# A recurrence's operand half loaded and half copied on chip, and a key product taken where its factor lies

## The chip, the cores and the metric

The kernel runs on one core of one Trainium2 chip. The metric is the device time of one execution in microseconds, the median of three runs.

## What is computed

The reference has three stages on float32 data. The change lies in the first, an attention with a recurrent state for each of 32 heads (4 batches of 8), 768 tokens and a head size of 40:

```python
for t in range(S):
    y[:, :, t] = np.einsum('bhd,bhde->bhe', rt, state)
    Sa = np.einsum('bhde,bhe->bhd', state, at)
    state_decay = state * wt[:, :, None, :] - np.einsum('bhd,bhe->bhde', Sa, bt)
    state = state_decay + np.einsum('bhd,bhe->bhde', vt, kt)
```

Its result, 3072 rows of 320, goes through a mixture of 8 experts of which each row takes two (routing by a noisy gate), and then through one feed-forward layer of width 2048.

## The kernel before

The recurrence is cut into chunks of 32 tokens (`C`), 24 in all (`NC`), and the 32 heads into two halves (`NP`), so that the main loop `chain(g)` has 48 steps: step g belongs to chunk g // 2 and half g % 2. A chunk's decays are folded into scaled operands, its inner dependence is a unit triangular matrix of 32 by 32 for each head, and the inverse of that matrix turns a chunk into a few matmuls.

Three generators run ahead of the chain and are interleaved with it at written-out times (`pump`). `prepare` makes a chunk's operands: `scale` forms running products of w on VectorE and multiplies a (`abd`) and k, b (`kb`) by them on GpSimd; `prods` forms the triangular matrices on TensorE, of which ScalarE takes one part to `lscr` in DRAM; `turns` transposes kb to token rows (`kn`, stored to DRAM as `knd`) and the decays to token rows (`EN`: a tile of 128 partitions holds two chunks, 64 partitions each, and for each partition two groups `ab` of heads). `scale_a` multiplies a in token rows by EN, into `AM`. `solve` takes four chunks (`GJ`) at a time: it loads lscr as `Lu`, inverts on VectorE with a few products on GpSimd, and stores the result as `tscr`. `apply` loads it as `Tbd` and multiplies AM by it, into `Zt`.

A step of the chain does `s_mm` (the state's part on TensorE with KB, scaled into the state tile ST two steps on by VectorE), `tr` (transposes of ST; ScalarE writes TRs and rows of KB), `u_mm` (Zt with ST of the next step, which ScalarE copies into ST), `y_mm` of the step before (the output, with KB and RR) and `rv_mm` (RR, masked by VectorE). KB is a tile for one chunk, two of them in turn. Its partitions 64 to 127 hold knd, for each half of the heads once for `s_mm` (index 0) and once again for `y_mm` (index 1).

Before the change `load_kb` (L494) fills both copies with one broadcast load of knd, issued in the even step of chunk i for chunk i + 1, after `y_mm`, which reads the buffer last. `load_at` (L251) loads a in the row order of AM, and `load_et` (L258) copies EN by two transfers into the same row order, so that `scale_a` (L265) is one multiply of 128 partitions; it runs two chunks behind `turns` (`LA`). `pair` (L201) loads 104 partitions of wa or kb, of which 40 to 63 are padding.

TensorE, VectorE, ScalarE and GpSimd run in the order in which the program is written. SyncE issues nearly all transfers; the order of its queue is planned by the framework from its own estimate of when each one can go, and each engine's queue is in order on the chip.

Of the kernel before, what the change touches and what calls it, by code (L numbers as in the profile page):

```python
# [11 lines left out]
F32 = mybir.dt.float32  # L12
# [17 lines left out]
NTB = 2  # L30
GJ = 4
RW = 64 + D
LA = 2


def layout_rec(inp):

    c = np.ascontiguousarray

    def heads_t(x):  # L40
        return x.reshape(NP, PR, 2, NC, C, D).transpose(3, 2, 5, 1, 0, 4)


    wa = np.zeros((NC, 2, 64, NW + 1 + 2 * PR * C), np.float32)
    w33 = np.ones((NC, 2, 64, PR, 2, C + 1), np.float32)
    w33[..., 0] = 0
    w33[:, :, :D, :, :, 1:] = heads_t(inp["w"])
    wa[..., :NW] = w33.reshape(NC, 2, 64, NW)
    wa[:, :, :D, NW + 1:] = heads_t(inp["a"]).reshape(NC, 2, D, -1)
    at = inp["a"].reshape(NP, PR, 2, NC, C, D).transpose(3, 2, 0, 4, 1, 5)  # L50
    kb = np.zeros((NC, 2, 64, PR, 2, 2, C), np.float32)
    for x, n in enumerate("kb"):
        kb[:, :, :D, :, :, x] = heads_t(inp[n])
    rt = inp["r"].reshape(NP, HH, NC, C, D).transpose(2, 4, 0, 1, 3)
    vn = np.zeros((NC, NP, C, HH, 64), np.float32)
    vn[..., :D] = inp["v"].reshape(NP, HH, NC, C, D).transpose(2, 0, 3, 1, 4)
    flat = lambda x: x.reshape(NC, 128, -1)
    rows = lambda x: c(flat(x)[:, :64 + D])
    return dict(wa=rows(wa), at=flat(c(at)), kb=flat(kb), r=c(heads_t(inp["r"])).reshape(NC, 2, D, -1), rt=c(rt).reshape(NC, D, -1), vn=vn)


UR = (96, 32)
# [2 lines left out]
class Rec:  # L65


    def __init__(self, ctx, nc, tc, ins, emit_x, ident, share, late):
        self.share, self.late = share, late
        self.nc, self.tc, self.ins, self.emit_x = nc, tc, ins, emit_x  # L70
        P = lambda n, b, **k: ctx.enter_context(tc.tile_pool(name=n, bufs=b, **k))
        self.one = P("rone", 1)
        self.p2, self.px = P("r2", 2), P("rx", 3)
        self.pet = P("ret", 1)
        self.pen = P("ren", 6)
        self.ptm, self.pwe = P("rtm", 2), P("rwe", 14)
        self.pp, self.py = P("rpp", 2, space=PS), P("rpy", 1, space=PS)

        self.cs = P("rcs", 4, space=PS)
        self.pd = P("rd", 2, space=bass.MemoryType.DRAM)  # L80
        self.pkn = P("rkn", 16, space=bass.MemoryType.DRAM)
        self.ident = ident
        self.scaled, self.lscr, self.tscr, self.Ec = {}, {}, {}, {}
        self.at = {}
        self.KN, self.ZT, self.EN, self.WE = {}, {}, {}, {}
        self.Y = {}
        self.seq = range(NC)
        self.extra, self.later, self.fresh = [], [], 0

    def consts_a(self):  # L90
        nc, one = self.nc, self.one
        self.w33, self.wa, self.a, self.abd, self.kb = [], [], [], [], []

        self.kbs = [one.tile([128, 4 * HH * D], F32, name=f"KB{i}") for i in range(2)]
        n = NW + 1 + 2 * PR * C
        for i in range(4):
            t = one.tile([128, n], F32, name=f"wa{i}") if i < 2 else self.kbs[0][:, n * (i - 2):n * (i - 1)]
            self.wa.append(t)
            self.w33.append(t[0:RW, 0:NW + 1])
            self.a.append(t[:, NW + 1:].rearrange("p (a b c) -> p a b c", a=PR, b=2))  # L100
        for i in range(3):
            self.kb.append(one.tile([128, PR, 2, 2, C], F32, name=f"kb{i}"))
        self.kb3 = self.share[:, 6 * PR * 96:6 * PR * 96 + 4 * PR * C].rearrange("p (a b s c) -> p a b s c", a=PR, b=2, s=2)
        for i in range(GJ):
            self.load_w(i)
            self.load(i)
        self.zero = one.tile([128, 64], F32, name="zero")
        nc.gpsimd.memset(self.zero, 0.0)
        self.d1 = one.tile([128, 2 * PR, C + 1], F32, name="d1")
        nc.gpsimd.memset(self.d1, 0.0)  # L110
        nc.gpsimd.memset(self.d1[:, :, 0:1], -1.0)
        self.d1b = []
        for i in range(2):
            t = one.tile([128, 2 * PR * (C + 1) + 1], F32, name=f"d1b{i}")
            nc.vector.memset(t, 0.0)
            self.d1b.append(t)
            self.abd.append(one.tile([128, PR, 2, 2, C], F32, name=f"abd{i}"))
            nc.vector.memset(self.abd[i], 0.0)
        make_identity(nc, self.ident)

        self.mml = one.tile([128, C], F32, name="mml")
        nc.gpsimd.memset(self.mml, 0.0)
        for q in range(4):
            m = self.mml[32 * q:32 * q + 32]
            nc.gpsimd.affine_select(out=m, in_=m, pattern=[[1, C]], compare_op=ALU.is_ge,
                                    fill=1.0, base=0, channel_multiplier=-1)
        self.AM = [self.share[:, i * PR * 96:(i + 1) * PR * 96].rearrange("p (a x) -> p a x", x=96)
                   for i in range(2 * GJ)]
# [70 lines left out]


    def pair(self, out, x, i, rows=RW):  # L201
        self.nc.sync.dma_start(out=out[0:rows], in_=self.ins[x][i, 0:rows])

    def load_w(self, i):
        self.pair(self.wa[self.wx(i)], "wa", i)
# [44 lines left out]

    def load_at(self, i):  # L251

        t = self.last_x if i == 1 else [self.px.tile([128, HH // 2, D], F32, name="X") for _ in range(2)] if i == 2 else [
            self.pet.tile([128, PR, D], F32, name=n) for n in ("AT", "ET")]
        self.nc.sync.dma_start(out=t[0], in_=self.ins["at"][i].rearrange("p (a x) -> p a x", x=D))
        self.at[i] = t

    def load_et(self, i):  # L258

        en, et = self.EN[i // 2], self.at[i][1]  # L260
        r = 64 * (i % 2)
        for ab in range(2):
            self.nc.sync.dma_start(out=et[64 * ab:64 * ab + 64], in_=en[r:r + 64, ab])

    def scale_a(self, i):  # L265
        self.ready = i + 1
        if i in self.at:
            at, et = self.at.pop(i)
            self.nc.gpsimd.tensor_tensor(out=self.AM[i % (2 * GJ)][:, :, 0:D], in0=at, in1=et, op=ALU.mult)

    def prods(self, i):
        self.made = i + 1
# [52 lines left out]
    def prepare(self):  # L325
# [3 lines left out]
        for i in range(GJ, n):  # L329
            pos = iter([i / GJ - 2 + s / (6 * GJ) if i >= 2 * GJ else self.early(start[i - GJ][s]) for s in range(6)])  # L330
            if i == GJ:
# [3 lines left out]
                self.decays(GJ - 1)  # L335
                for _ in self.turns(GJ - 1):
                    pass
                self.gaps(6, 2)
                self.decays(i)
            sc = iter(())  # L340
            yield next(pos)
            if i + 1 < n:
                sc = self.scale(i + 1)
                next(sc)
            if i == GJ:
                self.load_et(1)
                self.load_at(3)
            yield next(pos)
            next(sc, None)
            if i == GJ:  # L350
                self.scale_a(1)
            if i + 1 < n:
                self.decays(i + 1)
            self.prods(i)
            self.mask(i)
            if i - LA >= GJ:
                self.scale_a(i - LA)
            if i + 2 < n:
                self.load(i + 2)
            for _ in self.turns(i):  # L360
                yield next(pos)
            if i == GJ:
                for x in range(2, GJ):
                    self.load_et(x)
                    self.scale_a(x)
            if i - LA + 1 >= GJ:
                self.load_at(i - LA + 1)
                self.load_et(i - LA + 1)
        for i in range(n - LA, n):
            yield (i + LA) / GJ - 2  # L370
            self.scale_a(i)
            if i + 1 < n:
                yield (i + LA + .5) / GJ - 2
                self.load_at(i + 1)
                self.load_et(i + 1)


    def solve(self):
# [113 lines left out]


    def load_kb(self, i):  # L494
        KB, kn = self.KB[i % 2], self.KN.pop(i)
        self.nc.sync.dma_start(out=KB.rearrange("p c x h d -> p x (c h d)")[64:128], in_=kn[:, None].to_broadcast([64, 2, 2 * HH * D]))

    def load_v(self, g):
        nc, ins = self.nc, self.ins
# [106 lines left out]
    def chain(self, g, fill):  # L606
        if g == 0:
            self.u_mm(0)
        if g < NG - 2:
# [3 lines left out]
                self.load_rbd(g // NP + 1)  # L613
            if g % NP and OPT['ra'] == 1 and g + 1 < NG:
                self.load_r(g // NP + 1)
            if g % NP and OPT['kb'] == 1 and g > 1:
                self.load_kb(g // NP + 1)
            self.s_mm(g)
        fill()
        trs = []  # L620
# [2 lines left out]
            fill()  # L623
        if g + 1 < NG:
            self.u_mm(g + 1)
        fill()
        for sg in range(2):
            if g:
                self.y_mm(g - 1, sg)
        if g + 2 < NG:  # L630
# [3 lines left out]
                self.load_r(g // NP + 1)  # L634
            if g % NP == 0 and OPT['rb'] == 1:
                self.load_rbd(g // NP + 1)
            if g % NP == 0 and g and OPT['kb'] == 0:
                self.load_kb(g // NP + 1)
        fill()
        self.rv_mm(g, trs)  # L640
        fill()
# [6 lines left out]
    def begin(self):  # L648
# [11 lines left out]
        for x in self.consts_c():  # L660
            pass
        self.setup()
        for i in range(GJ):
            self.mask(i)
        for i in range(GJ - 1):
            if i > 1:
                self.decays(i)
            for _ in self.turns(i):
                pass
            if i == 0:  # L670
                self.load_at(0)
                self.load_et(0)
                self.scale_a(0)
                self.load_v(0)
                self.load_r(0)
                self.load_rbd(0)
# [5 lines left out]
            else:  # L682
# [2 lines left out]
                for _ in self.fill_kb(1):  # L685
                    pass
                self.load_kb(1)
        for i in range(1, 3):
            self.load_at(i)

    def run(self):
        nc = self.nc
# [1046 lines left out]
```

## Time and profile before

| what | us |
|---|---|
| median of three runs | 1428.05 (1428.04 to 1430.09) |
| the profiled execution | 1428.0 |
| its span, first to last instruction | 1426.2 |
| start, to the first s_mm | 123.9 |
| recurrence with its chain | 123.9 to 597 |
| experts and feed-forward layer | 597 to 1426.2 |

Over the span TensorE is busy 83%, VectorE 60%, ScalarE 47% and GpSimd 44%, at a mean granted TensorE clock of 0.905. From 597 us on TensorE is busy for 772.90 of 829.20 us, up to there for a good two thirds. The busy shares are means over stages with different limits; what is read below is the recurrence alone. A row of a timeline has the start, the busy time, the instruction, and in brackets the idle time ahead of it with what ended it.

### The profile page before, as it was taken

To read this page: it belongs to the slowest core of one execution; us is meant where nothing else is said; L and a number is where in the kernel's file an instruction comes from. 1 tells how busy PE (TensorE), PEld (TensorE's weight loads), DVE (VectorE), ACT (ScalarE), POOL (GpSimd) and SP (SyncE) were. 2 spreads that over 40 slices of the span, in tenths; PEclk is the share of its full clock that TensorE was granted. 3 is DMA by queue.
4 is the path that set the end of the run, shared out by engine and by line. 5 is a ranking of instruction groups with operands and counts; after the bars stand their busy time and mean duration, and the time that the engine had idled before them with its cause. 6 is when DMAs were issued, how large, how long until landed. Compare 5 with 4: busy or idle time off the path is not lost. (4 is left out here: it accounts for less than half of the span.)

```text
span 1426.2 us, 33947 instructions
## 1 busy us (share of the span) xinstructions
PE 1190.7 (83%) x13902; PEld 1135.5 (80%) x13902; DVE 861.2 (60%) x1570; ACT 664.0 (47%) x1419; POOL 623.1 (44%) x556
## 2 busy tenths in 40 slices
PE   3425778878787886885999999999888999999998
PEld 2325767767686775775999999998888999999998
DVE  8475837667493733362867876775236665556653
ACT  3423535545444433531443442442237666676664
POOL 4553734645262524162334544443045554454431
PEclk9557878988878888897999999999989999999999
DMA  6644667667755764424435545644245111110000
GB/s 152 156 132 129 162 152 193 177 149 182 178 132 114 127 111 85 141 77 133 128 104 179 163 148 179 204 142 148 66 114 155 29 36 32 29 47 10 15 15 20
DMA packets 147308, 165.64 MB, mean 116 GB/s; under 512 B 70294, under 2 KB 118422, under 8 KB 147126
## 3 DMA queue, kind: packets, MB, share of 16 engines
q1 hardware_dynamic: 136438, 140.85, 37.8%
q0 software_dynamic: 10688, 22.32, 5.8%
q8 instruction: 120, 1.97, 0.6%
q14 instruction: 62, 0.51, 0.1%
HBM read 116.06 MB, written 43.12 MB: 112 GB/s over the span
## 5 line engine op out<-in xcount | busy, mean ns | idle before, releaser
L1611 POOL TENSOR_TENSOR gl<-fh,gh 128x1024 fp32r<-128x1024 f32 x46 | 131.0, 2878 | 105.2 <-ACT gh L1627 101.9
L1253 PE MATMUL ph<-xh,w1h 128*128 128x256 f32 (+1 forms) x576 | 163.3, 296 | 12.0 <-issue 6.7
L1253 PE MATMUL ph<-xl,w1h 128*128 128x256 f32 (+1 forms) x576 | 162.5, 295 | 0.2
L1579 PE MATMUL fps<-fxh,ih 128*128 128x256 f32 x576 | 156.2, 286 | 1.4 <-DVE fh L1581 1.4
L1579 PE MATMUL fps<-fxl,ih 128*128 128x256 f32 x576 | 153.8, 281 | 0.5 <-DVE fxl L1109 0.3
L1610 DVE TENSOR_TENSOR fh<-fh,fp 128x1024 f32<-128x1024 f32 x48 | 95.0, 2014 | 60.3 <-ACT fp L1609 56.6
L1273 PE MATMUL py<-w2h,hh 128*128 128x320 f32 x400 | 129.2, 323 | 2.4 <-ACT hh L1105 1.6
L1107 DVE SCALAR_TENSOR_TENSOR hl<-ph,hh 128x512 fp32r<-128x512 f32 (+1 forms) x104 | 69.0, 665 | 103.0 <-ACT hh L1105 87.4
L1273 PE MATMUL py<-w2h,hl 128*128 128x320 f32 x400 | 125.7, 314 | 3.8 <-DVE hl L1107 3.6
L1273 PE MATMUL py<-w2l,hh 128*128 128x320 f32 x400 | 125.3, 313 | 2.0 <-DVE w2l L1109 2.0
L1253 PEld LDWEIGHTS ph<-xh,w1h 128*128 128x128 f32 x576 | 114.1, 198 | 13.3 <-issue 9.2
L1253 PEld LDWEIGHTS ph<-xl,w1h 128*128 128x128 f32 x576 | 114.3, 198 | 0.6 <-DVE xl L1109 0.6
L1641 PE MATMUL fpy<-oh,gl 128*128 128x320 f32 x384 | 114.6, 310 | 0.0
L1641 PE MATMUL fpy<-oh,gh 128*128 128x320 f32 x384 | 114.3, 310 | 0.0
L1641 PE MATMUL fpy<-ol,gh 128*128 128x320 f32 x384 | 113.9, 308 | 0.0
L1253 PE MATMUL ph<-xh,w1l 128*128 128x256 f32 (+1 forms) x384 | 112.9, 294 | 0.0
L1581 DVE COPY fh<-fps 128x512 f32<-128x512 f32 x96 | 64.6, 689 | 79.6 <-ACT fp L1580 73.7
L1579 PEld LDWEIGHTS fps<-fxh,ih 128*128 128x128 f32 x576 | 108.9, 189 | 1.8 <-DVE fh L1581 1.7
L1579 PEld LDWEIGHTS fps<-fxl,ih 128*128 128x128 f32 x576 | 109.0, 189 | 1.1 <-DVE fxl L1109 1.1
L1579 PE MATMUL fps<-fxh,il 128*128 128x256 f32 x384 | 107.7, 281 | 0.0
L1105 ACT ACTIVATE hh<-ph 128x512 fp32r<-128x512 f32 (+1 forms) x104 | 59.7, 580 | 98.7 <-PE ph L1253 91.8
L235 POOL TENSOR_TENSOR abd<-wa,E 40x512 f32<-40x512 f32 x40 | 64.4, 1609 | 66.7 <-issue 28.6
(276 smaller groups left out, 3306.4 us busy)
## 6 DMA issues: line engine op xcount, KB each, us to landing
KB<-knd SPq DMA_DIRECT2D x24, 640.0 KB
share<-in_w_dram SPq DMA_DIRECT2D x8, 1280.0 KB
wa<-in_wa_dram SPq DMA_DIRECT2D x22, 422.9 KB
kb<-in_kb_dram SPq DMA_DIRECT2D x20, 416.0 KB
share<-in_w_dram SPq DMA_DIRECT2D x8, 1024.0 KB
knd<-kn SPq DMA_DIRECT2D x24, 320.0 KB
yb<-y SPq DMA_DIRECT2D x22, 320.0 KB
ST<-in_vn_dram SPq DMA_DIRECT2D x48, 128.0 KB
```

What stands on the lines that cost most here:

```text
L235: (nc.vector if i <= OPT['nd'] else nc.gpsimd).tensor_tensor(out=abd[r, :, :, ab], in0=a[r], in1=E[r, :, :, 0:C], op=ALU.mult)
L1105: nc.scalar.activation(out=hi, in_=src, func=AF.Relu if relu else AF.Copy)
L1107: nc.vector.scalar_tensor_tensor(out=lo, in0=src, scalar=0.0, in1=hi.bitcast(F32), op0=ALU.max, op1=ALU.subtract)
L1253: nc.tensor.matmul(ph[:, m % c], lhsT=a, rhs=b, start=(q == 0), stop=(q == len(ops) - 1))
L1273: nc.tensor.matmul(py, lhsT=a[:, m, ts], rhs=b[:, m], start=(m == 0 and q == 0), stop=(m == FC - 1 and q == 2))
L1579: nc.tensor.matmul(ph[:, i], lhsT=a, rhs=b, start=(q == 0), stop=(q == len(ops) - 1))
L1581: nc.vector.tensor_copy(h[:, 2 * m2:2 * m2 + 2], ph)
L1610: mul = lambda s: nc.vector.tensor_tensor(out=h[:, s], in0=h[:, s], in1=p[:, s], op=ALU.mult)
L1611: low = lambda s: (nc.vector if last and s.start % 8 else nc.gpsimd).tensor_tensor(out=gl[:, s], in0=h[:, s], in1=gh[:, s].bitcast(F32), o ...
L1641: nc.tensor.matmul(py, lhsT=a[:, m, ts], rhs=w[:, m], start=(q == 0), stop=(q == len(ops) - 1))
```

## The change

Four edits. (1) `load_kb` loads one copy of knd into half 0 of KB, 320 KB in place of 640; `copy_kb`, new, has ScalarE copy it to half 1 in every step, after `u_mm`; behind the copy of a chunk's second step comes the load for the chunk after next, into the same buffer. (2) a in token rows is laid out as EN is, so `scale_a` multiplies in EN's own 64 partitions, in two instructions that write 64 partitions of AM each; the ET transfers are gone. (3) `scale_a(i)` follows `turns(i)` directly and not two chunks later, also in the start; the load of a for chunk i + 2 comes right behind it. (4) From chunk 4 on, wa and kb are loaded as two transfers of 40 partitions, without the padding.

```diff
-    at = inp["a"].reshape(NP, PR, 2, NC, C, D).transpose(3, 2, 0, 4, 1, 5)
+    at = inp["a"].reshape(NP, PR, 2, NC, C, D).transpose(3, 0, 4, 2, 1, 5)
...
+        self.AT = one.tile([128, 2, PR, D], F32, name="AT")
...
     def pair(self, out, x, i, rows=RW):
-        self.nc.sync.dma_start(out=out[0:rows], in_=self.ins[x][i, 0:rows])
+
+        for r in (slice(0, rows),) if i < GJ else (slice(0, D), slice(64, RW)):
+            self.nc.sync.dma_start(out=out[r], in_=self.ins[x][i, r])
...
     def load_at(self, i):
 
-        t = self.last_x if i == 1 else [self.px.tile([128, HH // 2, D], F32, name="X") for _ in range(2)] if i == 2 else [
-            self.pet.tile([128, PR, D], F32, name=n) for n in ("AT", "ET")]
-        self.nc.sync.dma_start(out=t[0], in_=self.ins["at"][i].rearrange("p (a x) -> p a x", x=D))
-        self.at[i] = t
-
-    def load_et(self, i):
-
-        en, et = self.EN[i // 2], self.at[i][1]
-        r = 64 * (i % 2)
+        if i < len(self.seq):
+            r = 64 * (i % 2)
+            self.nc.sync.dma_start(out=self.AT[r:r + 64].rearrange("p b a x -> p (b a x)"), in_=self.ins["at"][i])
+
+    def scale_a(self, i):
+
+        self.ready = i + 1
+        en, r = self.EN[i // 2], slice(64 * (i % 2), 64 * (i % 2) + 64)
         for ab in range(2):
-            self.nc.sync.dma_start(out=et[64 * ab:64 * ab + 64], in_=en[r:r + 64, ab])
-
-    def scale_a(self, i):
-        self.ready = i + 1
-        if i in self.at:
-            at, et = self.at.pop(i)
-            self.nc.gpsimd.tensor_tensor(out=self.AM[i % (2 * GJ)][:, :, 0:D], in0=at, in1=et, op=ALU.mult)
+            self.nc.gpsimd.tensor_tensor(out=self.AM[i % (2 * GJ)][64 * ab:64 * ab + 64, :, 0:D], in0=self.AT[r, ab], in1=en[r, ab], op=ALU.mult)
+        self.load_at(i + 2)
...
             self.prods(i)
             self.mask(i)
-            if i - LA >= GJ:
-                self.scale_a(i - LA)
             if i + 2 < n:
                 self.load(i + 2)
             for _ in self.turns(i):
                 yield next(pos)
...
-            if i - LA + 1 >= GJ:
-                self.load_at(i - LA + 1)
-                self.load_et(i - LA + 1)
-        for i in range(n - LA, n):
-            yield (i + LA) / GJ - 2
             self.scale_a(i)
...
     def load_kb(self, i):
+
         KB, kn = self.KB[i % 2], self.KN.pop(i)
-        self.nc.sync.dma_start(out=KB.rearrange("p c x h d -> p x (c h d)")[64:128], in_=kn[:, None].to_broadcast([64, 2, 2 * HH * D]))
+        self.nc.sync.dma_start(out=KB[64:128, :, 0].rearrange("p c h d -> p c (h d)"), in_=kn.rearrange("p (c x) -> p c x", c=2))
+
+    def copy_kb(self, g):
+        t = self.KB[(g // NP) % 2][64:128, g % NP]
+        self.nc.scalar.copy(out=t[:, 1], in_=t[:, 0])
...
         if g + 1 < NG:
             self.u_mm(g + 1)
+        self.copy_kb(g)
+        if g % NP and g // NP + 2 < NC:
+            self.load_kb(g // NP + 2)
         fill()
...
-            if g % NP == 0 and g and OPT['kb'] == 0:
-                self.load_kb(g // NP + 1)
...
         self.setup()
+        for i in range(2):
+            self.load_at(i)
         for i in range(GJ):
             self.mask(i)
         for i in range(GJ - 1):
...
             for _ in self.turns(i):
                 pass
+            self.scale_a(i)
             if i == 0:
-                self.load_at(0)
-                self.load_et(0)
-                self.scale_a(0)
```

## Rows read from the trace of the kernel before

**Rows 1.** Busy time by stretch: start and end, length, busy (instructions), clock, DMA share, GB/s.

```profile
123.90:174.00 50.10, 40.72 (x902) 36.61 (x903) 45.45 (x63) 27.98 (x82) 30.02 (x16) 0.90 0.53 134
174.00:220.00 46.00, 34.55 (x682) 31.37 (x682) 11.87 (x19) 19.65 (x60) 18.56 (x15) 0.78 0.61 158
220.00:263.80 43.80, 36.62 (x796) 33.16 (x793) 42.30 (x58) 25.26 (x74) 27.20 (x16) 0.92 0.73 180
263.80:298.70 34.90, 25.61 (x563) 23.39 (x563) 12.68 (x19) 16.88 (x50) 13.79 (x10) 0.85 0.68 173
298.70:344.70 46.00, 36.46 (x745) 33.35 (x740) 41.99 (x58) 23.18 (x68) 26.01 (x17) 0.85 0.69 165
344.70:382.70 38.00, 32.27 (x684) 29.09 (x682) 12.75 (x19) 20.48 (x63) 14.65 (x11) 0.87 0.68 177
382.70:436.40 53.70, 42.17 (x795) 38.69 (x795) 51.90 (x93) 23.75 (x71) 28.45 (x18) 0.78 0.56 137
525.00:550.00 25.00, 23.63 (x574) 21.53 (x573) 14.46 (x55) 14.68 (x45) 2.03 (x3) 1.00 0.62 141
```

The five busy times are those of TensorE's matmuls, its weight loads, VectorE, ScalarE and GpSimd.

**Rows 2.** TensorE's waits, 125 to 560 us: total, times, longest.

```profile
PE cs L561 <- DMA KB<-knd: 43.3, 12, 6.3
```

**Rows 3.** The same wait in three stretches: 174:220, 263.8:298.7, 344.7:382.7.

```profile
PE cs L561 <- DMA KB<-knd: 11.3, 2, 6.3
...
PE cs L561 <- DMA KB<-knd: 6.8, 2, 3.9
...
PE cs L561 <- DMA KB<-knd: 5.0, 2, 2.7
```

**Rows 4.** VectorE's waits, 125 to 560 us.

```profile
DVE tm L439 <- DMA Lu<-lscr: 37.4, 4, 10.5
```

**Rows 5.** SyncE in order of time, 272 to 300 us: start, length, issue.

```profile
277.28 0.38 SPq L289 DMA_DIRECT2D lscr<-Ls  x1
...
278.75 0.64 SPq L496 DMA_DIRECT2D KB<-knd  x1
279.49 0.55 SPq L309 DMA_DIRECT2D knd<-kn  x1
...
293.54 1.15 SPq L263 DMA_DIRECT2D ET<-EN  x2
294.73 0.58 SPq L411 DMA_DIRECT2D Lu<-lscr  x1
```

**Rows 6.** TensorE in order of time, the s_mm that this KB load releases.

```profile
288.52 0.81 PE L561 MATMUL cs<-ST,KB 128*40 128x40 f32 x32 [2.93 <-DMA KB<-knd]
```

**Rows 7.** SyncE's own waits, 125 to 560 us.

```profile
SPq L263 <- DMA knd<-kn: 26.2, 10, 4.2
```

**Rows 8.** VectorE in order of time in the start, 0 to 135 us.

```profile
71.97 1.26 DVE L224 TENSOR_TENSOR_SCAN E<-wa,d 104x528 f32<-104x528 f32 x1 [10.60 <-DMA wa<-in_wa_dram]
...
93.79 2.33 DVE L454 TENSOR_REDUCE Tt<-tm 128x64 f32<-128x1024 f32 x2
```

**Rows 9.** GpSimd in order of time in the start, 0 to 135 us.

```profile
79.32 0.86 POOL L269 TENSOR_TENSOR share<-lx,lx 128x320 f32<-128x320 f32 x1 [10.64 <-DMA lx<-EN]
...
89.94 1.43 POOL L269 TENSOR_TENSOR share<-X 128x320 f32<-128x320 f32 x1 [9.08 <-DMA X<-EN]
```

**Rows 10.** SyncE in order of time in the start, 0 to 135 us.

```profile
101.43 0.34 SPq L202 DMA_DIRECT2D wa<-in_wa_dram  x1
...
103.60 1.48 SPq L488 DMA_DIRECT2D tscr<-Tt  x1
```

**Rows 11.** Transfers by issue: count and size of one.

```profile
KB<-knd SPq DMA_DIRECT2D x24, 640.0 KB
```

**Rows 12.** Two tiles' instructions: ns of the shortest, median and longest, first and last start, shape.

```profile
L169 ACT ACTIVATE KB<-ident x4: 719/736/737, 38.5 to 49.4; 40x640 f32<-40x640 f32 x4
...
L269 POOL TENSOR_TENSOR share<-AT,ET x22: 851/864/2527, 45.8 to 475.5; 128x320 f32<-128x320 f32 x22
```

**Rows 13.** GpSimd's waits, 125 to 560 us.

```profile
POOL share L269 <- DMA ET<-EN: 54.0, 11, 17.0
```

## What I expected of the change

> **What bounds the kernel now.** I read the busy time by stretch first, cut where VectorE's triangular solves begin and end [rows 1]. From 597 us on TensorE is the bound and the change touches nothing there; that part only shifts. Up to 597 us no engine is full, so shares of busy time say little. What they do say: in a solve (123.9, 220.0, 298.7 and 382.7 us on) VectorE is busy for nearly the whole stretch, between solves it is nearly free, and there TensorE's granted clock is lowest (0.78, 0.85, 0.87, against 0.90 to 0.92 in the first two solves). I call these stretches *in a solve* and *between solves*.
>
> The second view was TensorE's waits. One stands above all others: the matmuls of s_mm on KB wait for the KB load, 43.3 us in 12 waits [rows 2]. By stretch, 11.3, 6.8 and 5.0 us of it lie between solves, two waits in each [rows 3]; the rest, 20.2 us, lies in solves.
>
> Third, what holds the next solve. At its head VectorE waits for the transfer Lu, 37.4 us in 4 solves [rows 4]. SyncE's order of time shows why [rows 5]: lscr of the last chunk of a group is issued at 277.28, Lu, which needs only that, at 294.73. Between them stand the 640 KB KB load (278.75) and knd (279.49), and the ET pair waits before it goes at 293.54. KB itself has landed when TensorE resumes at 288.52 [rows 6], 9.8 us after its issue. The waits of SyncE say on what ET stood: the landing of the knd store, which ET does not read, 26.2 us in 10 waits [rows 7]. So SyncE admits only so many transfers in flight, and a slow one holds those behind it.
>
> Fourth, the start. VectorE has a hole of 10.60 us until wa of chunk 6 lands at 71.97, and ends the first solve at 93.79 + 2.33 = 96.12 [rows 8]. GpSimd waits 10.64 and 9.08 us for ET copies [rows 9]. SyncE issues tscr, the solve's result, only at 103.60, behind a wa load that goes at 101.43 [rows 10]: that load overwrites what GpSimd's delayed abd multiply reads.
>
> **The change part by part.** The sum is made against the profiled execution, 1428.0 us, whose span is 1426.2; the median of the three runs is 1428.05, so both are the same time.
>
> *KB loads.* The load halves (640 KB to 320 KB [rows 11]) and is issued 0.6 of a step into the odd step of chunk i for chunk i+2, so it has 2.4 steps; before it was issued three quarters into the even step before its use and had 1.25. A solve covers four chunks, eight steps, and from one to the next it is 78.7 us (220.0 to 298.7), so a step is some 9.8 us and the lead some 23 us, against the 9.8 us that a load twice as big took. I cost the KB wait at nothing from the third chunk on. What is late next differs by place.
>
> Between solves the first wait of each stretch (6.3, 3.9, and 5.0 - 2.7 = 2.3 us, by their order) stands ahead of the products that feed the next solve: 12.5 us go. The second (5.0, 2.9, 2.7) falls while Lu is under way, and Lu is late next. Its path loses the ET pair's issue, 1.15 us, and 320 KB ahead of it: 328 KB in thousands at 173 GB/s is 1.9 us. So 3.0 us a stretch, 9.1 in three; together 21.6, with ends 12.5 (Lu no earlier) and 23.1 (all of [rows 3]).
>
> In the solves only VectorE's idle time can be won: 50.1 - 45.45, 43.8 - 42.3, 46.0 - 41.99 and 53.7 - 51.9 make 12.0 us [rows 1]. KB is most of what TensorE waits for there, but the idle time is not all its doing; I take 8, ends 0 and 12.0. The fourth Lu, in the stretch after 436 us, comes 3.0 earlier as well.
>
> The clock: between solves TensorE's 34.55, 25.61 and 32.27 busy us at 0.92 in place of 0.78, 0.85 and 0.87 would be 5.3, 1.9 and 1.8 shorter, 9.0 in all [rows 1]. Part of that work would then wait for something else: I take 4, ends 0 and 9.
>
> *The copies.* 48 ScalarE copies of 64x640 come in. The nearest row is ScalarE's 40x640 fill of the same tile, 0.74 us [rows 12]; 48 make 35 us, which is the upper end, the lower is 0. Each stands behind the ST copies that release the next step, and its input has landed, because s_mm read it earlier in the step. ScalarE is busy about half of each stretch [rows 1], so I let them hide, except where it is busiest and the steps are short (525 to 550 us: 14.68 of 25). For these I take a tenth of the upper end, rounded: 3 us lost. Behind each copy on SyncE hangs the next KB load, which before hung on TensorE's y_mm; the lead above covers it.
>
> *scale_a and AT.* One GpSimd multiply of 128x320, 0.86 us, becomes two of 64x320 [rows 12]. The other end of that price is half, by partitions; I take 0.86 each, since elements per partition are unchanged, and so 0.86 more for each of 24 chunks, 21 us. GpSimd waits 54.0 us for ET in 11 waits [rows 13], and these now end when ScalarE has written EN, before any transfer. I take 0 for this edit in the steady part, ends -5 and +21. AT's load takes the place of the old one in count, but it now waits for GpSimd's scale_a of two chunks before; it has two chunks, some 40 us, of lead, and what stands behind it on SyncE is the next rival.
>
> *The start.* With no ET, GpSimd's 10.64 + 9.08 us of waits go, the abd multiply no longer holds wa, and tscr can be issued when the solve ends: 103.60 - 96.12 = 7.5 us. Ahead of the awaited wa there are two KB loads with 320 KB less each: 655 thousand bytes at 173 GB/s make 3.8 us of the 10.60.
>
> *Padding.* From chunk 4 on wa and kb leave out 24 of 104 rows, in two issues each in place of one; the two ET issues that go make up for them on SyncE. By bytes, two kb and one wa load (rows of 1,024 and 1,041 floats) up to VectorE's hole lose 24 rows of about 4.1 thousand bytes each, 296 thousand or 1.7 us. No row tells how the rows of a transfer are spread, so the ends are 0 and 1.7, and I take the middle, 0.8. Later it is hidden. The start is 12.1 us in all, ends 3.8 and 10.6 + 7.5 = 18.1.
>
> The Trainium skill speaks against the padding edit: the page "DMA: Bandwidth & Descriptors", section "Why a DMA increments its semaphore by 16 and not by 1", lets a transfer use the largest number of DMA engines up to 16 that divides its rows. By it 104 rows go over 13 engines, 8 rows each, and two transfers of 40 over the same 10, again 4 + 4 = 8 each, so the busiest engine gains nothing and the sum would be 0.8 us smaller. No run here shows it yet.
>
> *Sum:* 21.6 + 8 + 3.0 + 4 + 12.1 - 3 = 45.7 us. 1428.0 - 45.7 = 1382.3, so 1382 us.
>
> **The rivals.**
> *A, the next wait takes over.* In flight limits and knd's slow landing remain, Lu comes no earlier, the solves keep their length. For it: SyncE's waits [rows 5, 7]. Against: the first waits between solves [rows 3] lie ahead of the products. Then only 12.5 between solves and the start's 12.1 remain, less 3 for the copies: 21.6, that is 1406 us.
> *B, slower: SyncE stands behind GpSimd.* The AT issue waits for scale_a, scale_a waits in GpSimd's order for EN and behind the solve's products, and Lu, Tbd, ST and KB stand behind AT. What GpSimd spent on ET was 54.0 / 11 = 4.9 us a wait; if SyncE inherits 3 us of that on the path in each of the 20 chunks of the steady part, 60 us go and the time is 1382 + 60 = 1442. It turns slower above 45.7 / 20 = 2.3 us a chunk. For it: SyncE does stand in order [rows 5, 10]. Against: SyncE's order is planned, and the AT load may go late by 40 us.
> *C, ScalarE becomes a link.* The copies stand between ST and the TRs copies of the next step; if all 48 count, 35 in place of 3: 1414 us. Against: ScalarE's half-idle stretches.
> *D, nothing that is late moves.* KB still lands late, because its issue stays where the planner puts it: 1428.
>
> **How the numbers follow.** My forecast, 1362 to 1402, gets 0.55; A 0.19; C 0.09; D 0.06; B 0.11. The range holds the forecast, A and C: below, all upper ends (23.1 + 12.0 + 3 + 9 + 18.1 = 65) give 1363 with free copies, and I go to 1354, because the Lu path may gain more than its bytes; above, 1416. Outside stay B, D and a little at the bottom. About 0.2%, 2.9 us, is what a measurement of this kernel tells from no change. Faster: forecast, A, C and a part of D and B, 0.86; the same 0.05; slower 0.09.
>
> **What would show it.** TensorE's wait for KB gone from the third chunk on, KB issues over 15 us ahead of their use; VectorE's wait for Lu remaining as the largest between solves; tscr issued within 2 us of the first solve's end, and the first s_mm some 12 us earlier than at present; about 35 us of new ScalarE work with no wait on it; no SyncE wait at AT. Wrong would be: a SyncE wait for GpSimd ahead of Lu or Tbd (B), s_mm or TRs waiting for the copy (C), Lu's hole grown by what KB's lost (A).

## The result

The changed kernel takes 1384.91 us, the median of four runs (1382.49 to 1387.08); the kernel before, run beside it, 1428.05. The ratio is 0.970, with an interval of 0.968 to 0.972: 43 us faster, where I had said 46 (1382). The profiled execution took 1384.45 us, its span is 1382.7 (before 1426.2), and the mean granted clock rose from 0.905 to 0.921. The time came out as forecast, the terms of the sum less closely. The cause that I gave for the largest wait did not hold: the experiments below show what it was, and with it a kernel that is faster than both.

### The profile page after: what moved, and what is told of

Same layout as the page of the kernel before. It is cut to its first block, busy times and chain, and to the rows that moved or that the text cites. A ratio compares the mean times of both kernels' runs of the same rounds, so it can differ in the third digit from the quotient of the medians.

```text
span 1382.7 us, 34101 instructions
## 1 busy us (share of the span) xinstructions
PE 1175.9 (85%) x13902; PEld 1119.6 (81%) x13902; DVE 856.0 (62%) x1570; ACT 697.9 (50%) x1467; POOL 657.7 (48%) x580
## 5 line engine op out<-in xcount | busy, mean ns | idle before, releaser
L1557 ACT ACTIVATE fp<-fps 128x512 f32<-128x512 f32 x96 | 55.9, 597 | 80.4 <-PE fps L1556 80.4
```

Source lines behind the costliest of these rows:

```text
L1557: nc.scalar.activation(out=p[:, 2 * m2:2 * m2 + 2], in_=ph, func=AF.Sigmoid, scale=-1.0)
```

## The profile after

The first view is the busy time by stretch, cut where VectorE's solves begin and end, as in [rows 1]: start and end, length, busy time (instructions) of TensorE's matmuls, its weight loads, VectorE, ScalarE and GpSimd, clock, DMA share, GB/s. The first, third, fifth and seventh rows are the solves.

```profile
116.00:164.60 48.60, 37.21 (x898) 32.95 (x894) 47.01 (x63) 30.63 (x84) 34.01 (x20) 0.99 0.45 121
164.60:200.10 35.50, 32.24 (x702) 29.43 (x702) 10.96 (x18) 25.52 (x72) 21.03 (x17) 0.91 0.66 178
200.10:242.70 42.60, 35.03 (x781) 31.25 (x783) 41.11 (x59) 26.02 (x74) 28.13 (x16) 0.92 0.51 138
242.70:273.70 31.00, 27.02 (x592) 24.48 (x588) 11.10 (x18) 19.44 (x55) 17.45 (x15) 0.89 0.63 174
273.70:315.10 41.40, 35.20 (x794) 31.39 (x795) 39.94 (x59) 27.85 (x78) 28.41 (x16) 0.96 0.53 142
315.10:346.50 31.40, 26.20 (x584) 23.55 (x585) 11.16 (x19) 19.06 (x55) 17.53 (x15) 0.89 0.60 167
346.50:400.00 53.50, 42.10 (x888) 38.37 (x889) 51.70 (x93) 28.69 (x79) 31.84 (x20) 0.84 0.36 99
400.00:424.50 24.50, 20.17 (x322) 17.96 (x310) 5.22 (x13) 11.76 (x34) 7.77 (x13) 0.84 0.56 132
```

The four solves sum to 186.1 us (before 193.6), the three stretches between them to 97.9 (before 118.9), and the one behind the fourth solve to 24.5 (before from 436.4 to the fifth solve's start at 467.7, 31.3). The first solve of the steady part starts at 116.0 in place of 123.9. These differences are 7.5, 21.0, 6.8 and 7.9 us, 43.2 of the 43.5 by which the span is shorter. From the fifth solve on nothing is left to find: 958.5 us before, 958.2 after.

TensorE's longest waits in 100 to 520 us (total, times, longest) have no KB among them; the 43.3 us of [rows 2] are gone.

```profile
PE pp L378 <- DMA Tbd<-tscr: 18.8, 5, 14.2
PE cs L528 <- DMA ST<-in_vn_dram: 9.6, 5, 2.9
PE cs L528 <- DVE RR L584: 9.2, 6, 2.7
```

The instructions on KB and GpSimd's multiplies by EN: ns of the shortest, median and longest, first and last start, shape. The copies cost about what the fill of [rows 12] cost (0.74 us), 0.72 us each; halving the partitions of scale_a did not halve its price, it stays 0.86 for each.

```profile
L476 ACT COPY KB<-KB x48: 721/722/725, 121.8 to 547.4; 64x640 f32<-64x640 f32 x48
L472 SPq DMA_DIRECT2D KB<-knd x24: 444/456/1437, 46.7 to 506.7; - x24
```
```profile
L262 POOL TENSOR_TENSOR share<-AT,EN x48: 851/864/2215, 40.4 to 418.1; 64x320 f32<-64x320 f32 x48
```

VectorE's wait for Lu still heads three of the four later solves. The row is of 125 to 560 us, as [rows 4] is: 29.9 in three stands against 37.4 in four, 10.0 each against 9.4. The fourth solve begins at 424.71, right behind VectorE's work on ST, without a wait for Lu.

```profile
DVE tm L414 <- DMA Lu<-lscr: 29.9, 3, 10.5
```

What holds Lu is seen on SyncE in order of time, the same place as [rows 5].

```profile
254.66 0.40 SPq L283 DMA_DIRECT2D lscr<-Ls  x1
...
256.56 0.55 SPq L303 DMA_DIRECT2D knd<-kn  x1
...
258.34 4.22 SPq L361 DMA_DIRECT2D Tbd<-tscr  x4
262.66 1.36 SPq L255 DMA_DIRECT2D AT<-in_at_dram  x1
266.42 0.46 SPq L472 DMA_DIRECT2D KB<-knd  x1
266.93 0.58 SPq L386 DMA_DIRECT2D Lu<-lscr  x1
```

From the issue of lscr to that of Lu it is 12.3 us, before 17.5. From there to the solve, which waits for Lu to land, it is now 6.8 us (266.93 to 273.7), before 4.0 (294.73 to 298.7). ET is gone from between them, but knd still stands there, and the KB load of the chunk after next, whose s_mm starts only at 279.1, goes ahead of Lu, for which VectorE waits. SyncE's own waits (100 to 520 us) name both, and a new one at AT:

```profile
SPq L255 <- POOL share L262: 23.9, 9, 3.8
SPq L472 <- ACT KB L476: 19.2, 6, 4.8
...
SPq L472 <- DMA knd<-kn: 13.2, 6, 2.3
...
SPq L361 <- DMA knd<-kn: 9.5, 2, 4.8
```

## The experiments

The chips differ: the kernel before took 1400.85, 1405.14 and 1401.69 us where the experiments ran. So kernels are compared by their ratio to the kernel before on the same chip, and differences in microseconds are against its median there. Where an expectation gives a time for the whole kernel, it counts from the 1428 and 1385 us of the first chip; read it as a difference from these.

**The KB edit alone.**

```diff
 (kernel before, with the new load_kb and copy_kb)
+        self.copy_kb(g)
+        if g % NP and g // NP + 2 < NC:
+            self.load_kb(g // NP + 2)
...
-            if g % NP == 0 and g and OPT['kb'] == 0:
-                self.load_kb(g // NP + 1)
```

> The kernel before with the KB edit alone: half load, ScalarE copy, load for the chunk after next behind the copy; ET transfers, scale_a two chunks behind, and padding stay. My theory (the KB wait stood on the path between solves, and the smaller load frees Lu and the start): 12.5 + 8 + 4 of the sum, 1.9 for each of four Lu loads, 3.8 in the start, less 3 for the copies, 33 us, so 1395 us; TensorE's wait for KB (43.3 us) gone, VectorE's wait for Lu no shorter than 37 us. Rival A (the next wait takes over): only the first waits and the start, less the copies, 13 us, so 1415. Rival that the other edits made the gain: 1420 or more.

Measured: 1376.51 us, ratio 0.983 (0.980 to 0.986), 24 us faster. TensorE's wait for KB is gone. VectorE's wait for Lu stays at 36.7 us in 4 (125 to 560 us), and SyncE's for knd at the ET pair (100 to 520 us) as it was:

```profile
SPq L263 <- DMA knd<-kn: 27.0, 10, 4.2
```

The gain lies between theory (33 us) and rival A (13). VectorE's 36.7 us for Lu, with ET still behind knd, make it likely that Lu gained less than I had given it; no run shows that by itself.

**Half the load, but at the old place.**

```diff
 (kernel before, with the new load_kb, of half 0 alone, and copy_kb)
+        self.copy_kb(g)
```

> The kernel before with half load and copy, but the load at its old place, in the even step of the chunk before: fewer bytes with the old lead. It tells bytes from lead. My theory (the lead matters): KB lands 2 to 5 us sooner than the 9.8 us it took, the waits of 3 to 6 us shrink to a total of 10 to 25 us and do not vanish; Lu and the start gain as in the KB edit alone; about 1410. Rival (bytes alone do it): the wait is gone as with the early load, and the time is that of the KB edit alone.

Measured: 1379.73 us, ratio 0.985 (0.983 to 0.988), 21 us faster; on the same chip as the run above, 3 us slower than that. Part of the wait is back:

```profile
PE cs L566 <- DMA KB<-knd: 18.9, 9, 5.2
```

The time is near my theory's (18 us) and the wait within its 10 to 25. So fewer bytes behind the old issue give most of the gain, and the early issue some 3 us, by medians; the intervals of the two ratios overlap.

**The ET edit alone.**

```diff
 (changed kernel, with load_kb, its place and the padded loads of before)
-        self.copy_kb(g)
...
+            if g % NP == 0 and g and OPT['kb'] == 0:
+                self.load_kb(g // NP + 1)
```

> The changed kernel with the old KB load (640 KB, old place, no copy) and with padding, so the ET edit alone: scale_a in EN's rows right behind turns, AT loads behind it. My theory: the start's 7.5 us, and 1.15 us of ET issue for each of four Lu loads, 12 us, so 1416; TensorE still waits some 40 us for KB. Rival B (SyncE behind GpSimd): the trace of the changed kernel shows SyncE waiting 23.9 us for scale_a in 9 waits; if that is on the path, 1428 - 12 + 24 = 1440.

Measured: 1389.78 us, ratio 0.992 (0.989 to 0.995), 11 us faster. My theory had 12 us, and a wait for KB that stays at some 40. The wait halves, though nothing was done to the load; that this is the ET pair gone from SyncE's order was not tried apart:

```profile
PE cs L534 <- DMA KB<-knd: 22.1, 9, 4.5
```

Rival B, in which this edit costs 60 us, falls.

**The AT load one chunk later.** The one sign of B in the changed kernel is SyncE's wait for GpSimd at AT, 23.9 us. Here AT is loaded where its buffer has long been free.

```diff
 (changed kernel)
-        self.load_at(i + 2)
+        if i < GJ:
+            self.load_at(i + 2)
...
+            if i > GJ:
+                self.load_at(i + 1)
```

> The changed kernel with the AT load of a chunk issued one chunk later, when scale_a of two chunks before has long ended, from chunk 6 on. SyncE waited 23.9 us for scale_a at AT in 9 waits. Rival B (these stand on the path): the wait goes and the time falls by 8 us or more. My theory (SyncE's wait ends before anything that is late): the wait goes and the time stays within 3 us of the changed kernel's.

Measured: 1362.77 us, ratio 0.970 (0.966 to 0.975); the changed kernel itself, run beside it:

> The changed kernel once more, beside the following three on one chip. Theory: a ratio of 0.970 to the kernel before, as in the first comparison. The kernel before was 1428 us there and 1401 on the chip of the four runs ahead of this one; if part of the gain lay in what differs between the chips, the ratio comes out at 0.975 or above.

Measured: 1361.18 us, ratio 0.971 (0.966 to 0.975), as on the first chip. The wait at AT, 27.7 us in the changed kernel on that chip, has left SyncE's list, and the time is the same. SyncE's longest waits (100 to 520 us) now begin so:

```profile
SPq L475 <- ACT KB L479: 26.8, 8, 4.6
SPq L304 <- ACT kn L302: 19.3, 6, 7.0
```

So these waits of a queue cost nothing: part of them went over to the KB load behind (14.6 to 26.8 us).

**Each copy twice.**

```diff
 (changed kernel)
-        self.nc.scalar.copy(out=t[:, 1], in_=t[:, 0])
+        for _ in range(2):
+            self.nc.scalar.copy(out=t[:, 1], in_=t[:, 0])
```

> The changed kernel with each KB copy done twice, 48 more ScalarE copies of 0.72 us, 35 us of work. My theory (the copies hide but for a tenth): 3 us slower than the changed kernel. Rival C (ScalarE is a link): 20 to 35 us slower. If nothing at all is on the path: within 1.5 us.

Measured: 1370.06 us, ratio 0.976 (0.972 to 0.980), 8.9 us above the changed kernel on the same chip. The row shows that it is 48 copies more at the same price:

```profile
L477 ACT COPY KB<-KB x96: 721/722/726, 122.4 to 538.4; 64x640 f32<-64x640 f32 x96
```

That is a quarter of their 35 us: three times my 3 us, and below rival C's 20 to 35. The intervals of the two ratios overlap, but the times of the two kernels on this chip do not (1358 to 1362 against 1368 to 1372).

**The padding, two ways.** First the changed kernel with the padded loads of 104 rows, then the kernel before with the padding edit alone.

```diff
-        for r in (slice(0, rows),) if i < GJ else (slice(0, D), slice(64, RW)):
-            self.nc.sync.dma_start(out=out[r], in_=self.ins[x][i, r])
+        self.nc.sync.dma_start(out=out[0:rows], in_=self.ins[x][i, 0:rows])
```

> The changed kernel with wa and kb loaded as before, 104 rows in one transfer, padding and all. My theory: 0.8 us slower by the bytes in the start alone, 1386, not to be told from the changed kernel's 1385. If the bytes count in every chunk: 24 of 104 rows of wa and kb are 197 thousand bytes, 1.1 us at 173 GB/s, for 18 chunks 20 us, so 1405. If the second issue of each load costs more than its bytes save: 36 issues of some 0.4 us, 14 us, so 1371.

> The kernel before with the padding edit alone: from chunk 4 on wa and kb go as two transfers of 40 rows in place of one of 104. My prediction's step gave it 0.8 us, so no change that can be measured (0.999 to 1.000). By the rule that a transfer uses the largest number of DMA engines up to 16 that divides its rows the busiest engine has 8 rows either way, so 0, or a little slower for 40 more issues on SyncE (1.000 to 1.003). The changed kernel with padded loads stood 0.7% above the changed kernel, on another chip; if that is the padding, 6 to 10 us (0.993 to 0.996).

Measured: the first 1368.49 us, ratio 0.977 (0.974 to 0.981); the second 1404.38 us, ratio 1.0024 (1.0003 to 1.0045). Alone the edit gains nothing; if anything, it costs some 3 us. The Trainium skill's rule in the page "DMA: Bandwidth & Descriptors", section "Why a DMA increments its semaphore by 16 and not by 1", which I had weighed against this edit, agrees with that 1.0024. The first run would give the edit 0.7% inside the changed kernel, but it ran on another chip than the runs of the changed kernel; whether the edit pays beside the others stays open. The first run also is the KB and ET edits together without the padding edit: 32 us faster than the kernel before on its chip.

**The knd store over more rows.** What is left on SyncE in the changed kernel is knd. In [rows 5] knd is issued at 279.49 and the ET pair that waits for it goes at 293.54: 14 us for 320 KB, while the KB load of 640 KB, issued just ahead, landed in 9.8. The store's destination is written with the two halves of the heads as its outer dimension, `"r (c x) -> c r x"`. The records of single packets in this trace show what the 14 us are: the store's 128 packets of 2560 bytes start at 286.6, when those of the KB load are nearly through, and end at 293.1. They come 20 in a microsecond at 0.102 us each, so two at a time.

What waits for the store need not use it: it is the eighth transfer issued behind it, whichever that is. Behind the store of 279.49 this is ET, behind the one of 259.55 it is ST, whose wait (259 to 279 us) and issue are:

```profile
SPq L501 <- DMA knd<-kn: 4.4, 1, 4.4
...
272.61 0.33 SPq L501 DMA_DIRECT2D ST<-in_vn_dram  x1
```

Behind 16 of the 17 stores issued from 126 to 447 us the eighth transfer goes within 0.6 us of the store's last packet. So SyncE goes on as if it had room for eight transfers under way; whether the chip or the framework sets that, no run shows.

Here knd is kept as 128 rows, as kn lies in its partitions; the KB load reads the same bytes.

```diff
 (changed kernel)
-        self.KN[i] = self.pkn.tile([64, 2 * HH * D], F32, name="knd")
-        ...dma_start(out=self.KN[i].rearrange("r (c x) -> c r x", c=2), in_=kn.rearrange("p h d -> p (h d)"))
+        self.KN[i] = self.pkn.tile([128, HH * D], F32, name="knd")
+        ...dma_start(out=self.KN[i], in_=kn.rearrange("p h d -> p (h d)"))
```

> The changed kernel with knd laid out in DRAM as 128 rows of 640 floats in place of 64 rows of two halves, so that the store's outermost run is 128 and not 2; the bytes and the run length stay. It tests what now holds Lu: SyncE waits for knd's landing (13.2 us at KB, 9.5 us at Tbd in the changed kernel), which took 10 to 14 us. Theory (the slow store holds the queue, and its few outermost runs make it slow): these waits go below 5 us, VectorE's waits for Lu (44.6 us) shrink by 10 or more, 8 to 20 us faster than the changed kernel. Rival (bytes in flight set the landing, or Lu waits for lscr itself): within 3 us of it.

Measured: 1333.77 us, ratio 0.951 (0.946 to 0.955), 27 us under the changed kernel on the same chip, more than the theory's 8 to 20. It is the fastest kernel of this study. SyncE no longer waits for knd at all, the first s_mm comes at 104.0 us (changed kernel 118.8 there), and the waits for Lu in 125 to 560 us shrink:

```profile
DVE tm L414 <- DMA Lu<-lscr: 16.1, 3, 6.7
```

From lscr to Lu it is now 8.7 us, in place of 12.3:

```profile
238.66 0.40 SPq L283 DMA_DIRECT2D lscr<-Ls  x1
...
241.11 0.38 SPq L303 DMA_DIRECT2D knd<-kn  x1
...
246.70 0.61 SPq L472 DMA_DIRECT2D KB<-knd  x1
247.36 0.58 SPq L386 DMA_DIRECT2D Lu<-lscr  x1
```

**The same store in the kernel before.** This asks what made the KB wait of 43.3 us: the size and place of the load, which the change treats, or the store ahead of it. Nothing else differs from the kernel before; KB is loaded in full, 640 KB, at its old place.

```diff
 (kernel before)
-        ...dma_start(out=self.KN[i].rearrange("r (c x) -> c r x", c=2), in_=kn.rearrange("p h d -> p (h d)"))
+        for c in range(2):
+            ...dma_start(out=self.KN[i][:, c * HH * D:c * HH * D + HH * D], in_=kn[64 * c:64 * c + 64].rearrange("p h d -> p (h d)"))
```

> The kernel before with one edit: the knd store goes as two transfers of 64 rows in place of one whose destination has the two halves outermost. Question: were the KB waits of before (43.3 us in 12) made by the size of the KB load or by the slow knd store ahead of it? Theory 1 (the store): the KB load follows a store that holds few DMA engines for long, so with a quick store KB lands in some 6 us in place of 9.8, most of the 43.3 us go, SyncE's wait of 26.2 us for knd goes, and the time falls by 20 to 35 us (0.976 to 0.986 of before). Theory 2 (the size): the 640 KB load and its late issue make the waits; over 30 of the 43.3 us stay and the time falls by under 8 us (over 0.994).

Measured: 1345.74 us, ratio 0.961 (0.956 to 0.966), 56 us faster than the kernel before. One store, split in two, gives more than the whole change. The KB wait, 125 to 560 us, here and, on the same chip, in the kernel before with the padding edit alone:

```profile
PE cs L562 <- DMA KB<-knd: 12.7, 7, 4.2
...
PE cs L563 <- DMA KB<-knd: 41.7, 13, 5.2
```

SyncE's waits for knd in 125 to 560 us, which in the kernel before are 50.2 (26.2 at ET [rows 7], 9.5 at ST, 7.9 at Tbd, 5.1 at tscr, 1.5 at Lu), shrink to 0.7:

```profile
SPq L255 <- DMA knd<-kn: 0.7, 2, 0.4
```

The load itself is hardly quicker. That of chunk 8 took 9.8 us from its issue to its s_mm [rows 5, 6], here 9.2:

```profile
239.59 0.62 SPq L497 DMA_DIRECT2D KB<-knd  x1
...
248.78 0.81 PE L562 MATMUL cs<-ST,KB 128*40 128x40 f32 x32 [1.26 <-DMA KB<-knd]
```

But SyncE comes to it earlier. Over the loads of chunks 4 to 16 the mean issue is 0.8 us behind the start of the s_mm one step ahead of the load's first use in the kernel before, and 0.4 us ahead of it here; from issue to use it is 10.2 us there and 9.8 here. Together these are 1.5 us a load, some 20 us over 13 loads, of the 30.6 us by which the wait shrinks; the rest was not taken apart.

and the hole for wa in the start (40 to 130 us), 10.60 us in [rows 8]:

```profile
DVE E L224 <- DMA wa<-in_wa_dram: 3.2, 1, 3.2
```

The first s_mm comes at 100.4 us in place of 124.2 (123.9 in the table is the start of the solve beside it). Theory 1 named the store, but not its way to the wait (KB does not land in 6 us; it is issued earlier), and its 20 to 35 us were too few: the same store also held the start.

**The quick store and the full KB load.** The changed kernel with the quick store, but KB loaded in full at its old place and no copies.

```diff
 (changed kernel, with the two stores of 64 rows as above)
-        self.copy_kb(g)
-        if g % NP and g // NP + 2 < NC:
-            self.load_kb(g // NP + 2)
...
+            if g % NP == 0 and g and OPT['kb'] == 0:
+                self.load_kb(g // NP + 1)
```

> The changed kernel with the quick knd store (two transfers of 64 rows), but with the full 640 KB load of KB at its old place and no ScalarE copies. Question: is the halving of KB still worth its copies once knd is quick? Theory 1 (the halving mainly hid the slow store): KB waits under 10 us, time as with the quick store and the half load (0.950 to 0.957 of before). Theory 2 (the size counts by itself): KB waits over 15 us, between solves most of all, and 0.962 to 0.975.

Measured: 1337.64 us, ratio 0.957 (0.954 to 0.960). The time is in the range of theory 1; the wait lies between the two theories (under 10, over 15) and is as in the run above:

```profile
PE cs L537 <- DMA KB<-knd: 13.1, 7, 3.9
```

Beside the run above, on the same chip, the ET and padding edits are worth 8 us. Against the kernel with half the load and copies (0.951, on another chip, its store one of 128 rows) it is 0.6% slower, with intervals that overlap: once the store is quick, halving KB is worth between nothing and some 9 us, where it gave 24 us alone. The 13 us of KB waits that remain are of the order of the 9 us that doubling the copies cost.

**The start: abd on VectorE.** In the changed kernel VectorE's work from its hole to the end of the first solve took 69.52 to 97.91, 28.4 us; before, 71.97 to 96.12, 24.2 us [rows 8]. I suspected GpSimd's work, which now lies beside it. Here the abd multiplies of chunks 4 to 7 are VectorE's.

```diff
 (changed kernel)
-OPT = dict(... nd=3, ...)
+OPT = dict(... nd=7, ...)
```

> The changed kernel with the abd multiplies of chunks 4 to 7, in the start, on VectorE in place of GpSimd (8 multiplies of 40x512). In the changed kernel VectorE's work from its hole for wa to the end of the first solve took 28.4 us, before 24.2. Theory 1 (VectorE and GpSimd slow each other): the two late chunks add 4 x 0.66 = 2.6 us to VectorE, GpSimd loses 6.47 + 5.39 us of work beside it, and VectorE's instructions lose the 4 us; the first solve ends 1 to 3 us earlier (95 to 97 us, the changed kernel 97.9) and the first s_mm with it. Theory 2 (no clash, chance or another cause): it ends 2 to 3 us later, at 100 to 101. Whole time: 0.967 to 0.972 of before under either.

Measured: 1367.32 us, ratio 0.978 (0.975 to 0.981). The hole ends at 70.11 and the solve at 101.80, 31.7 us, of which the abd multiplies behind the hole take 1.38 + 2.56; 27.8 are left against 28.4. By the time of the solve's end theory 2 is nearer: moving abd away freed nothing. By the rows the clash is there, but with whatever GpSimd does. The same scan of 104x528 takes 1.26 us at 70.11 and 3.23 at 81.25, while GpSimd multiplies kb from 80.15 to 83.37 (VectorE first, then GpSimd):

```profile
70.11 1.26 DVE L224 TENSOR_TENSOR_SCAN E<-wa,d 104x528 f32<-104x528 f32 x1 [10.18 <-DMA wa<-in_wa_dram]
...
81.25 3.23 DVE L224 TENSOR_TENSOR_SCAN E<-wa,d 104x528 f32<-104x528 f32 x1
```
```profile
80.15 3.22 POOL L238 TENSOR_TENSOR kb<-kb,R 104x1024 f32<-104x1024 f32 x1 [8.12 <-DVE P L429]
```

The scan ends 1.1 us after GpSimd's multiply does, a little less than its own time, as if it had stood still while GpSimd worked. The Trainium skill's page "SBUF — State Buffer", section "SBUF: two separate sides", has it so: an instruction of VectorE with two operands in SBUF and one of GpSimd that reads SBUF lock one pair of ports against each other, for a whole instruction. The two rows agree. Why the whole kernel stood at 0.978, outside both theories, is open; its last s_mm starts at 510.6 us, that of the changed kernel on another chip at 512.6; the profiled execution, at 1360.48 us, is also the fastest of its four.

## Why the prediction was right, and where it was not

**Between solves:** the step that first waits lie ahead of the products held. 21.6 us and most of the 4 us for the clock were forecast, 21.0 measured; the clock rose to 0.91, 0.89 and 0.89 from 0.78, 0.85 and 0.87 [rows 1], a little short of the 0.92 that I had put in. That the clock is lowest between solves I had read from the first two solves alone: the third and fourth had 0.85 and 0.78 [rows 1], and have 0.96 and 0.84 now.

**Lu:** I gave 3.0 us a stretch. From the issue of lscr at 277.28 [rows 5] to the solve at 298.7 [rows 1] it was 21.4 us; after, from 254.66 to 273.7, 19.0: 2.4 us. Lu was issued 5.2 us sooner behind lscr and landed 2.8 us later behind its issue; I had not put in that second part. The fourth stretch gained 6.8 in place of 3.0.

**Inside the solves:** 8 forecast, 7.5 measured.

**The start:** 12.1 forecast, 7.9 measured. Its first part held: tscr is issued at 97.94, at the end of the solve (97.91), in place of 103.60 behind it [rows 8, 10]. The other 4.6 us failed. The hole for wa ends 2.45 us earlier, at 69.52, but the solve ends 1.8 us later. Against that, the next solve starts 18.1 us behind tscr (97.94 to 116.0) in place of 20.3 (103.60 to 123.9), 2.2 us that no term held. The step that failed passed the earlier end of the hole on whole to the end of the solve, and took the end of GpSimd's 9.08 us wait [rows 9] for a gain alone: while GpSimd sat idle, to 89.94, VectorE had its scans in 1.24 and 1.26 us. In the kernel before, VectorE:

```profile
81.87 1.24 DVE L224 TENSOR_TENSOR_SCAN E<-wa,d 104x528 f32<-104x528 f32 x1
...
83.50 1.26 DVE L228 TENSOR_TENSOR_SCAN R<-wa,d1b 104x529 f32<-104x529 f32 x1
...
91.98 1.88 DVE L451 TENSOR_TENSOR tm<-Tt,P 128x1024 f32<-128x1024 f32 x1
```

and in the changed kernel, VectorE and then GpSimd:

```profile
69.52 1.47 DVE L224 TENSOR_TENSOR_SCAN E<-wa,d 104x528 f32<-104x528 f32 x1 [12.07 <-DMA wa<-in_wa_dram]
...
81.08 2.70 DVE L228 TENSOR_TENSOR_SCAN R<-wa,d1b 104x529 f32<-104x529 f32 x1
...
91.93 3.73 DVE L426 TENSOR_TENSOR tm<-Tt,P 128x1024 f32<-128x1024 f32 x1
95.57 2.34 DVE L429 TENSOR_REDUCE Tt<-tm 128x64 f32<-128x1024 f32 x2
```
```profile
71.71 6.47 POOL L235 TENSOR_TENSOR abd<-wa,E 40x512 f32<-40x512 f32 x2
79.54 3.12 POOL L238 TENSOR_TENSOR kb<-kb,R 104x1024 f32<-104x1024 f32 x1 [1.36 <-DVE tm L426]
...
91.72 2.18 POOL L238 TENSOR_TENSOR kb<-kb,R 104x1024 f32<-104x1024 f32 x1
```

The scan at 81.08 and the product at 91.93 took 1.44 and 1.85 us longer than their like before, each with a GpSimd multiply beside it that had begun first. Before, the product at 91.98 had begun ahead of GpSimd's abd multiplies at 92.16: it took its 1.88 us, and those two took 3.94, where one alone at 98.99 took 1.16.

**The copies:** 3 us forecast as lost. TensorE waits for none of them, but doubling them cost 8.9. If the first 48 cost what the second 48 did, which no run shows, the term was some 6 us too small.

**scale_a and AT:** 0 forecast, and the ET edit alone gave 11 us, which the terms of the start and of Lu contain. I had written that no SyncE wait would stand at AT; 23.9 us of them do, which was one of my signs of being wrong. The consequence that I feared from such a wait did not come, as the later AT load shows.

**Padding:** 0.8 forecast; alone it gains nothing.

**The sum:** 45.7 forecast, 43.5 measured. That it came within 2.2 us is in part luck: the start and the stretches between solves gave 4 to 5 us less each than forecast, the fourth stretch 3.8 more. The edits alone give 24 and 11 and cost 3, some 32 us, and the KB and ET edits together, which is the changed kernel with padded loads, give 32 as well. So the ten more of the whole change lie in the padding edit beside the others or between the chips, which no run tells apart. In the trace with padded loads the first s_mm comes at 121.7 us, in the two of the changed kernel at 115.4 and 118.8.

**The cause of the KB wait** is where the argument, and not its result, was wrong. I costed the wait by the load's size and lead, and saw in SyncE's waits for knd [rows 7] a rival's obstacle alone. The quick store in the kernel before takes 43.3 us of KB waits to 12.7 without touching the load. The load did not read that store: chunk 8's, issued at 278.75, reads the knd stored at 145.73. Nor was a store under way ahead of it: the one of 259.55 had landed at 272.2, and the next was issued behind it. It was late because SyncE, having stood on the store of the chunk before, came to it late. The change gives the load enough lead to sit that out, if not the 23 us that I had counted (13 to 22 us for chunks 3 to 18). It does not remove the store, so SyncE's waits for knd move to KB and Tbd, and the quick store on top gave another 27 us. The rule that I had applied to the padding bears on this store too: by the Trainium skill's page "DMA: Bandwidth & Descriptors", in the same section, a destination whose outer dimension is 2 lets a transfer use two DMA engines. The trace agrees: the store's packets go two at a time, 20 in a microsecond, and as two stores of 64 rows 52 to 114 in the busiest one. The 27 and 56 us of the two kernels with 128 or 64 outer rows agree as well.

**Rivals:** A's obstacle was real (Lu at 10.0 us a solve), its price was not; B and C are refuted at their prices; D did not occur.

## What to carry to other kernels

When a load lands late, look at what stands ahead of it and what it reads before paying for fewer bytes or more lead: a queue's waits named by one slow transfer (26.2 us in ten waits for a store of 320 KB) point to that transfer's access pattern, even where what waits does not use it. An engine's wait that goes away lets its work run beside other engines' work, and if two of them hold each other up, part of the gain goes there. A wait of a queue costs only if what stands behind it is late.

## What the runs showed of the hardware that I had not expected

A store of 320 KB to DRAM with a destination of two outer rows moved its packets two at a time, in 6.5 to 7.4 us, and landed 9 to 15 us behind its issue; as two stores of 64 rows it landed 4 to 9 us behind it, and with 64 or 128 outer rows it all but left SyncE's waits. The eighth transfer behind such a store waited for it. A VectorE scan of 1.26 us takes 2.7 to 3.2 us beside a GpSimd multiply that began first. And a difference of chips: the steps 40 to 45 of the recurrence take 49.2 us before and 48.1 after on the first chip, but 27 to 28 us in every kernel on the others, nearly all of the difference in the last of these steps (25 us against 4), so absolute times of this kernel compare only on one chip; what makes it is open.
